# Dense output projection from layer two, and filler targets of 1.76 and 3.0 in turn, in a four-layer attention kernel

## The chip, the cores and the metric

The kernel runs on one core of a Trainium2 chip. The time is device microseconds of one launch, from the first instruction of the program to its end; the median of several runs is compared. A profile of one execution comes with it. The engines are named as the profile names them: PE (TensorE matmuls; PEld is its weight load), DVE (VectorE), ACT (ScalarE), POOL (GpSimd) and SP (SyncE, which here only issues DMAs).

## The reference

One sequence of 2048 rows and 640 columns goes through four residual attention layers. Layers one and three use the weights `A` and a sliding window of 256 keys; layers two and four use the weights `B` and attend to all 2048 keys, in both directions. There are 32 heads of 20 columns.

```python
def _A_ref(x, wqkv, wo):                 # _B_ref: the same without the mask
    qkv = (x @ wqkv).reshape(B, S, 3, H, Dh)...
    scores = jnp.einsum("bhqd,bhkd->bhqk", q, k) * (Dh ** -0.5)
    mask = (idx[:, None] - idx[None, :] >= 0) & (idx[:, None] - idx[None, :] < W)
    p = _softmax(jnp.where(mask, scores, -1e9))
    o = jnp.einsum("bhqk,bhkd->bhqd", p, v)
    return o.transpose(0, 2, 1, 3).reshape(B, S, D) @ wo

x = A_x
x = x + _A_ref(_layernorm(x), A_wqkv, A_wo)
x = x + _B_ref(_layernorm(x), B_wqkv, B_wo)
x = x + _A_ref(_layernorm(x), A_wqkv, A_wo)
x = x + _B_ref(_layernorm(x), B_wqkv, B_wo)
```

## The kernel before

**Tiling.** The 2048 rows are four chunks `c` of 512. The 32 heads are eight groups `g` of four; a head's 20 rows of Q and K lie at the partitions 32j to 32j+19, so that the four heads of a group use the four row strips of the PE array. A *unit* is one chunk's queries of one group in one layer (in the code layers count from `l` = 0). A unit's scores come out transposed, keys on partitions: one *bank* is 128 keys by 512 queries of one head. A *tile* is up to three banks (two and three in turn in layer one and the first part of layer two), and is one step of the main loop: PE computes the scores of a tile into one of two PSUM regions (line 1244), ACT takes the exponential (line 1275), and PE multiplies groups of four banks, two or three steps old, with V (line 1308) into the PSUM bank `op`. V has a 21st column of ones, so the 21st row of a head's strip in `op` is the sum of its weights. There are 1635 steps.

**Tail of a unit.** When a unit's last PV group is emitted, DVE copies `op` to `oT` (line 830) and the task `t_tail` is started: PE gathers the sums (line 1011), DVE takes reciprocals and splits them in two bf16 halves, PE transposes them (line 1028), PE spreads them over the strips (line 1039), and DVE multiplies (line 1043) into the slot `on[:, g, :]` of the chunk's tile `on`. Steps are left between these by `yield ("wait", 2)`. In `on`, as in `op`, a head has 32 partitions, of which 20 hold values; so a chunk's output projection contracts over eight blocks of 128 partitions, and the weights `wop` are laid out the same way by `load_wop` (lines 129 to 132), with zeros between, written once at the start by `t_zeros`.

**Output projection.** After the tail of group 7, `t_out(l, c)` (line 517 on) runs for each of four blocks of 128 rows and two halves of 320 columns eight matmuls (line 532), and DVE adds the result to the residual `x_sb` (line 541). `wop` is one buffer: when the next projection in the fixed order `out_seq` needs the other weights, the end of `t_out` loads them with four DMAs on SP. In the last chunk of layer four the first six groups are projected early by `t_before_last` (line 563), and `t_out` adds the last two.

**Background tasks.** Norms (`t_ln`), projections to Q, K and V (`project`, line 353; `t_v`, line 446), output projections and tails are Python generators. Each step of the main loop grants credit, `pump` (called with the rate of `rate(t)`) advances the tasks by it in order of need, and one PSUM bank (bank 6 after the first part of layer two) serves all of them. Their DMAs and instructions stand in each engine's queue in the order of the steps. SP's queue holds the loads of later units (one for V, four each for Q and K, or eight for a windowed unit) and the loads of `wop`; POOL's holds the loads of the projection weights and the stores of Q, K and V.

**Filler matmuls.** `keep_clock` (after `pump`, in each step) issues `unread`: a matmul of 128 by 128 by 512 into the free bank, whose result nothing reads (line 611). It does so while `state["heat"]`, what the tasks of this step have added, plus a carry of up to 3.0, is below `state["least"]`. A full projection matmul adds 1.0, an output matmul 0.64. The target is set once per step, and is zero from the second chunk of layer four on:

```python
warmth = 1.76 if state["unit"] >= woven else 1.0
state["least"] = warmth * n_b / 3 if state["unit"] < index[3, 1, 0, None] else 0.0
```

`woven` is the first unit of layer two, which begins among layer one's. When the free bank was used in the same step, no filler is issued. Two fillers stand ahead of each transpose group in the norms of the first two layers.

Of the kernel before, what the change touches and what calls it, by code (L numbers as in the profile page):

```python
# [12 lines left out]
ALU = mybir.AluOpType  # L13
ACT = mybir.ActivationFunctionType

P = 128
# [3 lines left out]
DH = 20  # L20
NT = S // P
KD = D // P
G = 8
C = 512
NC = S // C
EPS = 1e-5
SCALE = DH ** -0.5
HD = D // 2
# [21 lines left out]
def kernel(  # L50
# [10 lines left out]
    nc = tc.nc  # L61
# [27 lines left out]
    wo_in = (A_wo, B_wo)  # L89
# [5 lines left out]
    wop = big.tile([P, G, D], BF16, name="wop", tag="wop")  # L95
# [13 lines left out]
    op = ps[:, 7, :]  # L109
# [10 lines left out]
    for h in range(2):  # L120
        for n in range(2):
            a = n * D + h * HD
# [3 lines left out]
        nc.sync.dma_start(out=x_sb[:, 4 * c : 4 * c + 4, :], in_=xin[:, 4 * c : 4 * c + 4, :])  # L126
    nc.sync.dma_start(out=wv_sb[1][:], in_=wq_view[1][:, :, 2 * D : 3 * D])

    def load_wop(w):
        v = wo_in[w].rearrange("(g j e) f -> j e g f", g=G, j=4)  # L130
        for j in range(4):
            nc.sync.dma_start(out=wop[32 * j : 32 * j + DH, :, :], in_=v[j])
# [3 lines left out]
        out=ident[:], in_=ident[:], compare_op=ALU.not_equal, fill=1.0,  # L136
# [6 lines left out]
    for m, b, ge in (  # L143
# [4 lines left out]
        v = masks[:, m, b * P : (b + 1) * P]  # L148
        nc.gpsimd.affine_select(
            out=v, in_=v, compare_op=ALU.is_ge if ge else ALU.is_gt, fill=0.0,  # L150
# [26 lines left out]
    state = {"tick": 0, "held": None, "credit": 0.0, "early": True, "act": True, "unit": 0, "heat": 0.0, "carry": 0.0, "least": 0.0}  # L177
# [339 lines left out]
    out_seq = [0] * 4 + [1, 0] * 4 + [1] * 4  # L517
    out_n = [0]

    def t_out(l, c):  # L520
        on = ons[l, c]
        last = (l, c) == (3, NC - 1)
        while last and "before_last" not in ready:
            yield ("wait", 1)
        assert out_seq[out_n[0]] == l % 2
        for qb in range(4):
            for i in range(2):
                mb = yield from take_m()
                yp = ps[:, mb, 0:HD]
                g0 = G - 2 if last else 0  # L530
                for g in range(g0, G):
                    nc.tensor.matmul(  # L532
                        yp, lhsT=on[:, g, qb * P : (qb + 1) * P],
                        rhs=wop[:, g, i * HD : (i + 1) * HD],
                        start=(g == g0), stop=(g == G - 1),
                    )
                    if g < G - 1:
                        yield ("hold", 0.14)
                xv = x_sb[:, 4 * c + qb, i * HD : (i + 1) * HD]
                had = part_o["t"][:, 2 * qb + i, 0:HD] if last else xv  # L540
                nc.vector.tensor_tensor(out=xv, in0=had, in1=yp, op=ALU.add)  # L541
                drop_m(mb)
                yield ("pe", 0.14)
            if l < 3:
                stats(l + 1, c, qb)
            else:
                nc.sync.dma_start(out=xout[:, 4 * c + qb, :], in_=x_sb[:, 4 * c + qb, :])
        ons.pop((l, c))
        ready.add(("out", l, c))
        ready.add(("x", l + 1, c))  # L550
        n = out_n[0] = out_n[0] + 1
        if n < len(out_seq) and out_seq[n] != out_seq[n - 1]:
            load_wop(out_seq[n])

    def t_before_last():

        on = ons[3, NC - 1]
        for qb in range(4):
            for i in range(2):
                mb = yield from take_m()  # L560
                yp = ps[:, mb, 0:HD]
                for g in range(G - 2):
                    nc.tensor.matmul(
                        yp, lhsT=on[:, g, qb * P : (qb + 1) * P],
                        rhs=wop[:, g, i * HD : (i + 1) * HD],
                        start=(g == 0), stop=(g == G - 3),
                    )
                    if g < G - 3:
                        yield ("hold", 0.14)
                xv = x_sb[:, 4 * (NC - 1) + qb, i * HD : (i + 1) * HD]  # L570
                nc.vector.tensor_tensor(
                    out=part_o["t"][:, 2 * qb + i, 0:HD], in0=xv, in1=yp, op=ALU.add
                )
                drop_m(mb)
                yield ("pe", 0.14)
        ready.add("before_last")
# [420 lines left out]
    def t_tail(l, c, g, on, oT):  # L997
        def fill(count):

            for n in range(count * ((l, c, g) == (3, NC - 1, G - 1))):  # L1000
                nc.tensor.matmul(
                    ps[:, 0, :], lhsT=ident[:], rhs=masks[:, 0, :], start=True, stop=True
                )

        yield ("wait", 2)
        fill(2)
        mb = yield from take_m()
        warm_bank(mb)
        zp = ps[:, mb, 0:16]
        for qb in range(4):  # L1010
            nc.tensor.matmul(
                zp[:, 4 * qb : 4 * qb + 4], lhsT=oT[:, qb * P : (qb + 1) * P],
                rhs=sel4[:], start=True, stop=True,
            )
        rz = rzp.tile([P, 16], F32, name="rz", tag="rz")
        nc.vector.reciprocal(out=rz[:], in_=zp)
        drop_m(mb)

        hl = rzp.tile([P, 2, 16], BF16, name="hl", tag="hl")
        nc.vector.tensor_copy(out=hl[:, 0, :], in_=rz[:])  # L1020
        nc.vector.tensor_tensor(out=hl[:, 1, :], in0=rz[:], in1=hl[:, 0, :], op=ALU.subtract)
        yield ("pe", 0.25)
        fill(3)
        yield ("wait", 2)
        mb = yield from take_m()
        warm_bank(mb)
        rp = ps[0:32, mb, :].bitcast(BF16)[:, 0:P]
        nc.tensor.transpose(out=rp, in_=hl[:].rearrange("p n r -> p (n r)"), identity=ident[:])
        rT = rzp.tile([32, P], BF16, name="rT", tag="rT")
        nc.vector.tensor_copy(out=rT[:], in_=rp)  # L1030
        drop_m(mb)
        yield ("pe", 0.1)
        fill(1)
        yield ("wait", 2 if state["tick"] < last_tick[0] else 1)
        mb = yield from take_m()
        warm_bank(mb)
        zb = ps[:, mb, :]
        for qb in range(4):
            nc.tensor.matmul(  # L1039
                zb[:, qb * P : (qb + 1) * P], lhsT=spread4[:, qb, :], rhs=rT[:],  # L1040
                start=True, stop=True,
            )
        nc.vector.tensor_tensor(out=on[:, g, :], in0=oT[:], in1=zb, op=ALU.mult)  # L1043
        drop_m(mb)
        yield ("pe", 0.3)
        fill(3)
        ready.add(("tail", l, c, g))
        if (l, c, g) == (3, NC - 1, G - 3):
            push("before_last", t_before_last(), 0, 8.0)
        if g == G - 1:  # L1050
            need = first_use(l + 1, c, 0) if l < 3 else len(units) + c
            push(("out", l, c), t_out(l, c), need, 9.0)
            if l < 3:
                push_layer(l + 1, c)
    def t_zeros():

        z = ka_all[:, G : G + 4, :].rearrange("p a b -> p (a b)")
        yield ("wait", 4)
        for n in range(2):
            nc.gpsimd.dma_start(  # L1060
                out=wop[:, 4 * n : 4 * n + 3, :].rearrange("p g f -> p (g f)"), in_=z[:, 0 : 3 * D]
            )
            nc.gpsimd.dma_start(out=wop[:, 4 * n + 3, :], in_=z[:, 0:D])
            yield ("wait", 1)
        load_wop(0)
        for t in (*kts, *qts):
            nc.gpsimd.dma_start(out=t[:], in_=z[:, 0 : t.shape[1]])
            yield ("wait", 1)
        ready.add("kts")
# [67 lines left out]
    with tc.manual_schedule():  # L1137
# [9 lines left out]
        woven = index[1, 0, 0, PARTS[1][0]]  # L1147
# [4 lines left out]
        n = 0  # L1152
# [54 lines left out]
        t = -1  # L1207
        ended = None
        closed = -2
        while ended is None or t < ended + 8:  # L1210
# [3 lines left out]
            if t < len(tiles) or banks:  # L1214
# [26 lines left out]
                for n in range(2):  # L1241
                    for i, (u, j, m, b0, subs, first, last, end) in enumerate(cur):
                        for kc, q0, qn, col in subs[n : n + 1]:
                            nc.tensor.matmul(  # L1244
                                sp[:, i, col * P : (col + qn) * P],
                                lhsT=u.k(kc, j), rhs=u.q(j, q0, qn), start=True, stop=True,
# [22 lines left out]
                i = 0  # L1269
                while i < n_b:  # L1270
                    b0 = cur[i][3]
                    k = i
                    while k < n_b and cur[k][3] == b0:
                        k += 1
                    nc.scalar.activation(  # L1275
                        out=pt[:, i:k, b0 * P :], in_=sp[:, i:k, b0 * P :],
                        func=ACT.Exp, scale=SCALE,
                    )
                    i = k
                for i, b in enumerate(cur):  # L1280
                    pts.append((t, pt, i, b))
                warmth = 1.76 if state["unit"] >= woven else 1.0
                state["least"] = warmth * n_b / 3 if state["unit"] < index[3, 1, 0, None] else 0.0
                load_ahead()
                r = rate(t)
# [6 lines left out]
            for n in range(2 if n_b == 0 or t > closed + 1 else 0):  # L1292
# [7 lines left out]
                subs, end = group[0][3][4], group[-1][3][7]  # L1300
                first, last = group[0][3][5:7]
# [3 lines left out]
                for m, (kc, q0, qn, col) in enumerate(subs):  # L1305
                    for _, pg, i, b in group:
                        j = b[1]
                        nc.tensor.matmul(  # L1308
                            op[32 * j : 32 * j + VW, q0 * P : (q0 + qn) * P],
                            lhsT=u.v(kc, j), rhs=pg[:, i, col * P : (col + qn) * P],  # L1310
                            start=(first and m == 0), stop=(last and m == len(subs) - 1),
                            skip_group_check=u.windowed,
                        )
                if end and u.aside:
                    pair = side_done(u)
                    for n, j in enumerate(u.aside):
# [15 lines left out]
            if t > 0 and masked is not None:  # L1332
                cur_, pt_ = masked
                i = 0
                while i < len(cur_):
# [4 lines left out]
                    if m is not None:  # L1340
# [44 lines left out]
```

## Time and profile before

| | |
|---|---|
| median of 3 runs (range) | 2338.6 us (2338.2 to 2338.93) |
| the profiled execution's time | 2338.93 us |
| its span, first to last instruction | 2337.2 us |
| mean granted clock of PE | 0.852 |
| exponentials, ACT line 1275, 128x1536 | 1366 records, 1886.3 us |
| scores, PE line 1244, 512 columns | 4008 records, 644.6 us |
| output projection, PE line 532 | 976 records, 165.5 us, 312 ns each |
| fillers, PE line 611 | 672 records (768 weight loads), 231.7 us, 393 ns each |
| tail's product, DVE line 1043 | 128 records, 87.5 us, 683 ns each |

The profile's page gives busy time by engine and in 40 slices of the span; PEclk is the clock that PE was granted, in tenths of full speed. A matmul's busy time holds its pipeline, so matmuls that follow each other overlap and their mean durations add to more than the time they take; start to start is the price. In the timeline a bracket gives the idle time before an instruction and what ended it. An engine's queue is in order: an instruction that waits holds up all behind it.

### The profile page before, as it was taken

How to read it: one execution, taken by the hardware profiler on the slowest of the kernel's cores; microseconds unless marked ns; L12 is line 12 of the kernel's file. 1: busy time of each engine (PE TensorE's matmuls, PEld its weight loads, DVE VectorE, ACT ScalarE, POOL GpSimd, SP SyncE). 2: the span in 40 equal slices, each digit the busy share in tenths (PEclk: the TensorE clock that was granted, in tenths of full speed). 3: DMA queues.
4: the chain of work that ended last, by engine and by line, in shares of the span. 5: the costliest groups of instructions: out<-in, count | busy, mean ns of one | idle time of the engine just before them, and what ended most of it. 6: DMA issues, size and time to landing. Idle time of an engine off the chain costs nothing.

```text
span 2337.2 us, 40427 instructions
## 1 busy us (share of the span) xinstructions
PE 1992.5 (85%) x15613; PEld 722.9 (31%) x15773; DVE 1464.3 (63%) x2724; ACT 2179.5 (93%) x1753; POOL 271.1 (12%) x445
## 2 busy tenths in 40 slices
PE   8899988888888888888888898888888888888887
PEld 3444333333223332323323333333322222222222
DVE  6677775426646666656667644452577777777772
ACT  7788989899999988999899999999999999999997
POOL 3332311200200112001120013001000000000000
PEclk9999999999989999999999999999855565556556
DMA  5232321321300223102231023112210010011100
GB/s 183 81 103 80 107 65 56 90 68 48 89 21 25 58 68 90 43 14 58 70 99 31 17 82 107 41 28 76 65 30 27 26 38 27 27 35 39 31 14 12
DMA packets 84881, 132.57 MB, mean 57 GB/s; under 512 B 19760, under 2 KB 60080, under 8 KB 84688
## 3 DMA queue, kind: packets, MB, share of 16 engines
q1 hardware_dynamic: 65472, 76.80, 11.9%
q0 software_dynamic: 19216, 53.17, 7.8%
q8 instruction: 124, 2.03, 0.4%
q14 instruction: 69, 0.57, 0.1%
HBM read 98.70 MB, written 27.79 MB: 54 GB/s over the span
## 4 chain that ended last, share of the span: by engine, by line
ACT 40%; PE 27%; issue 17%; DVE 13%; DMA 1%; POOL 1%; ACTq 0%; SPq 0%; DVEq 0%; POOLq 0%; another core or an unknown queue 0%
ACT pt L1275 39%; PE ps L1244 7%; PE ps L353 5%; PE ps L532 4%; PE ps L1308 4%; DVE pt L1344 3%; PE ps L446 2%; PE ps L611 2%; DVE on L1043 1%; DVE st L304 1%; DMA wqk<-in_B_wqkv_dram 1%; ACT ka L1275 1%; DVE oT L830 1%; DVE raw_o L878 1%; PE ps L410 1%
## 5 line engine op out<-in xcount | busy, mean ns | idle before, releaser
L1275 ACT ACTIVATE pt<-ps 128x1536 bf16<-128x1536 f32 (+2 forms) x1641 | 2100.9, 1492 | 115.2 <-PE ps L1244 104.6
L1244 PE MATMUL ps<-qt,kt 32*128 32x512 bf16 x4008 | 644.6, 457 | 197.1 <-ACT pt L1275 164.2
L1308 PE MATMUL ps<-pt,vt 128*21 128x512 bf16 x3860 | 469.2, 458 | 5.1 <-issue 2.2
L1244 PEld LDWEIGHTS <-kt 32*128 32x128 bf16 x4008 | 191.0, 93 | 615.1 <-issue 592.0
L1344 DVE TENSOR_TENSOR pt<-pt,masks 128x1024 bf16<-128x1024 bf16 (+5 forms) x403 | 239.0, 626 | 131.5 <-ACT pt L1275 131.0
L611 PE MATMUL ps<-masks,ident 128*128 128x512 bf16 x672 | 231.7, 393 | 27.0 <-DVE rT L1030 9.6
L353 PE MATMUL ps<-xnT,wqk 128*128 128x512 bf16 x767 | 211.4, 388 | 24.8 <-DMA wqk<-in_B_wqkv_dram 4.2
L1308 PEld LDWEIGHTS <-vt 128*21 128x21 bf16 x3960 | 100.0, 90 | 319.1 <-issue 309.7
L304 DVE CAST st<-ps 128x512 bf16<-128x512 f32 x127 | 87.8, 691 | 154.4 <-PE ps L353 150.8
L532 PE MATMUL ps<-wop,on 128*128 128x320 bf16 x976 | 165.5, 312 | 6.9 <-DVE x_sb L541 2.5
L1244 PE MATMUL ps<-qa,ka 32*128 32x384 bf16 (+2 forms) x1408 | 116.8, 275 | 33.9 <-ACT pt L1275 28.8
L878 DVE TENSOR_SCALAR xnT<-ps 128x512 int32<-128x512 f32 x88 | 60.8, 691 | 106.3 <-PE ps L871 105.9
L1043 DVE TENSOR_TENSOR on<-oT,ps 128x512 bf16<-128x512 bf16 x128 | 87.5, 683 | 59.5 <-PE ps L1039 59.2
L830 DVE CAST oT<-ps 128x512 bf16<-128x512 f32 x112 | 76.9, 686 | 70.8 <-PE ps L1308 45.4
L446 PE MATMUL ps<-wv,xnT 128*128 128x320 bf16 x640 | 111.9, 309 | 7.0 <-DVE va L304 1.6
L541 DVE TENSOR_TENSOR x_sb<-x_sb,ps 128x320 bf16<-128x320 bf16 x120 | 57.9, 482 | 95.1 <-PE ps L532 94.9
L532 PEld LDWEIGHTS <-on 128*128 128x128 bf16 x976 | 90.2, 101 | 71.4 <-issue 38.4
L353 PEld LDWEIGHTS <-wqk 128*128 128x128 bf16 x830 | 71.3, 98 | 114.0 <-issue 49.2
L387 POOL TENSOR_SCALAR rstd<-mv 128x4 f32<-128x4 f32 x15 | 4.0, 265 | 815.6 <-DVE mv L374 815.5
L611 PEld LDWEIGHTS <-ident 128*128 128x128 bf16 x768 | 56.4, 97 | 126.2 <-issue 123.0
L1308 PE MATMUL ps<-pt,va 128*21 128x384 bf16 (+2 forms) x1408 | 77.6, 281 | 4.9 <-DVE pt L1344 2.9
L1244 PEld LDWEIGHTS <-ka 32*128 32x128 bf16 x1408 | 44.4, 92 | 101.2 <-issue 92.7
(107 smaller groups left out, 1790.9 us busy)
## 6 DMA issues: line engine op xcount, KB each, us to landing
vt<-v_d SPq DMA_DIRECT2D x48, 336.0 KB
kt<-k_d SPq DMA_DIRECT2D x192, 80.0 KB
wqk<-in_B_wqkv_dram POOLq DMA_DIRECT2D x80, 160.0 KB, 3.8
wqk<-in_A_wqkv_dram POOLq DMA_DIRECT2D x70, 160.0 KB, 3.3
k_d<-st POOLq DMA_DIRECT2D x75, 128.0 KB, 2.1
q_d<-st POOLq DMA_DIRECT2D x75, 128.0 KB, 2.1
qt<-q_d SPq DMA_DIRECT2D x384, 20.0 KB
v_d<-vs POOLq DMA_DIRECT2D x16, 336.0 KB, 3.1
```

The costliest lines, as they stand in the source:

```text
L304: nc.vector.tensor_copy(out=out_, in_=in_)
L353: nc.tensor.matmul(pq, lhsT=wt[:, dc, :], rhs=xt[:, dc, :], start=(dc == 0), stop=(dc == KD - 1),)
L446: nc.tensor.matmul(pv, lhsT=xt[:, dc, i * P : (i + 1) * P], rhs=wv_sb[l % 2][:, dc, h * HD : (h + 1) * HD], start=(dc == 0), stop=(dc == K ...
L532: nc.tensor.matmul(yp, lhsT=on[:, g, qb * P : (qb + 1) * P], rhs=wop[:, g, i * HD : (i + 1) * HD], start=(g == g0), stop=(g == G - 1),)
L611: nc.tensor.matmul(ps[:, b, :], lhsT=ident[:], rhs=masks[:, 0, :], start=True, stop=True)
L830: nc.vector.tensor_copy(out=oT[:], in_=op)
L878: V.tensor_scalar(out=xi.bitcast(I32)[:, i * C : (i + 1) * C], in0=side["psum"], scalar1=SCALE * LOG2E * E23, scalar2=127.0 * E23, op0=ALU ...
L1043: nc.vector.tensor_tensor(out=on[:, g, :], in0=oT[:], in1=zb, op=ALU.mult)
L1244: nc.tensor.matmul(sp[:, i, col * P : (col + qn) * P], lhsT=u.k(kc, j), rhs=u.q(j, q0, qn), start=True, stop=True,)
L1275: nc.scalar.activation(out=pt[:, i:k, b0 * P :], in_=sp[:, i:k, b0 * P :], func=ACT.Exp, scale=SCALE,)
L1308: nc.tensor.matmul(op[32 * j : 32 * j + VW, q0 * P : (q0 + qn) * P], lhsT=u.v(kc, j), rhs=pg[:, i, col * P : (col + qn) * P], start=(first ...
L1344: nc.vector.tensor_tensor(out=pt_[:, i:k, b0 * P :], in0=pt_[:, i:k, b0 * P :], in1=mv_, op=ALU.mult,)
```

## The change

From layer two on, the output projection contracts over five dense blocks of 128 rows in place of eight padded ones. `load_wop` gets a flag: dense weights come in one DMA of 128 partitions; once, after layer one, four further DMAs bring groups 6 and 7 of `B_wo` in the padded layout to the blocks 6 and 7. In `t_tail` the product is written to one of three scratch slots (5 to 7 of `on`), and two steps later SP copies each of the four heads' 20 rows to its dense place in the slots 0 to 4; a head that crosses a block's border takes two copies. The last two groups of the last chunk stay padded, and `t_before_last` contracts over four blocks (the last of 96 rows) in place of six. In `keep_clock`'s target, 1.76 becomes 3.0 on odd steps. A tail counts as done two steps later where it copies.

```diff
+    def packed(l, c):
+        return l > 0
+
-    def load_wop(w):
+    def load_wop(w, dense):
+        if dense:
+            nc.sync.dma_start(out=wop[:, 0:KD, :], in_=wo_in[w].rearrange("(b p) f -> p b f", p=P))
+            if w and out_n[0] == 4:
+                v = wo_in[w].rearrange("(g j e) f -> j e g f", g=G, j=4)
+                for j in range(4):
+                    nc.sync.dma_start(
+                        out=wop[32 * j : 32 * j + DH, G - 2 : G, :], in_=v[j][:, G - 2 : G, :]
+                    )
+            return
...
+        dense = packed(l, c) and not last
+        a, b = (0, KD) if dense else (G - 2 if last else 0, G)
         for qb in range(4):
             for i in range(2):
                 mb = yield from take_m()
                 yp = ps[:, mb, 0:HD]
-                g0 = G - 2 if last else 0
-                for g in range(g0, G):
+                for g in range(a, b):
                     nc.tensor.matmul(
                         yp, lhsT=on[:, g, qb * P : (qb + 1) * P],
                         rhs=wop[:, g, i * HD : (i + 1) * HD],
-                        start=(g == g0), stop=(g == G - 1),
+                        start=(g == a), stop=(g == b - 1),
                     )
...
-        if n < len(out_seq) and out_seq[n] != out_seq[n - 1]:
-            load_wop(out_seq[n])
+        if n < len(out_seq) and (n == 4 or out_seq[n] != out_seq[n - 1]):
+            load_wop(out_seq[n], n >= 4)
...
-                for g in range(G - 2):
+                for b in range(4):
+                    n = min(P, (G - 2) * 80 - b * P)
                     nc.tensor.matmul(
-                        yp, lhsT=on[:, g, qb * P : (qb + 1) * P],
-                        rhs=wop[:, g, i * HD : (i + 1) * HD],
-                        start=(g == 0), stop=(g == G - 3),
+                        yp, lhsT=on[0:n, b, qb * P : (qb + 1) * P],
+                        rhs=wop[0:n, b, i * HD : (i + 1) * HD],
+                        start=(b == 0), stop=(b == 3),
                     )
...
-        nc.vector.tensor_tensor(out=on[:, g, :], in0=oT[:], in1=zb, op=ALU.mult)
+        end = (l, c) == (3, NC - 1) and g >= G - 2
+        spread = packed(l, c) and not end
+        nu = on[:, 5 + g % 3 if spread else g, :]
+        nc.vector.tensor_tensor(out=nu, in0=oT[:], in1=zb, op=ALU.mult)
         drop_m(mb)
         yield ("pe", 0.3)
         fill(3)
+        if spread:
+            yield ("wait", 2)
+            for j in range(4):
+                r, a = (4 * g + j) * DH, 0
+                while a < DH:
+                    b, o = divmod(r + a, P)
+                    n = min(DH - a, P - o)
+                    nc.sync.dma_start(
+                        out=on[o : o + n, b, :], in_=nu[32 * j + a : 32 * j + a + n, :]
+                    )
+                    a += n
...
-        load_wop(0)
+        load_wop(0, False)
...
-                warmth = 1.76 if state["unit"] >= woven else 1.0
+                warmth = (3.0 if t % 2 else 1.76) if state["unit"] >= woven else 1.0
```

By line of the two built programs, the matmuls of the output projection falls from 976 to 712, the early part of the last one from 48 to 32, and the fillers rise from 768 to 1035. SP's list gains 423 copies within `on` and loses 23 loads of `wop`. The other counts are the same.

More of the change, by code (lines that the diff above doesn't have):

```diff
@@ L534, in t_out @@
                         rhs=wop[:, g, i * HD : (i + 1) * HD],
-                        start=(g == g0), stop=(g == G - 1),
+                        start=(g == a), stop=(g == b - 1),
                     )
-                    if g < G - 1:
+                    if g < b - 1:
                         yield ("hold", 0.14)
@@ L561, in t_before_last @@
                 yp = ps[:, mb, 0:HD]
-                for g in range(G - 2):
+                for b in range(4):
+                    n = min(P, (G - 2) * 80 - b * P)
                     nc.tensor.matmul(
-                        yp, lhsT=on[:, g, qb * P : (qb + 1) * P],
-                        rhs=wop[:, g, i * HD : (i + 1) * HD],
-                        start=(g == 0), stop=(g == G - 3),
+                        yp, lhsT=on[0:n, b, qb * P : (qb + 1) * P],
+                        rhs=wop[0:n, b, i * HD : (i + 1) * HD],
+                        start=(b == 0), stop=(b == 3),
                     )
-                    if g < G - 3:
+                    if b < 3:
                         yield ("hold", 0.14)
```

## The prediction

> **What bounds the kernel now.** I read the page's busy shares first, then its slices, then the busy time of each engine by stretches.
>
> ```profile
> PE 1992.5 (85%) x15613; PEld 722.9 (31%) x15773; DVE 1464.3 (63%) x2724; ACT 2179.5 (93%) x1753; POOL 271.1 (12%) x445
> ...
> ACT  7788989899999988999899999999999999999997
> ...
> PEclk9999999999989999999999999999855565556556
> ```
>
> ScalarE (ACT), which takes the exponentials, is the bound: 2179.5 of 2337.2 us. The change leaves its instructions as they are, so it can only move the 157.7 us in which ACT idles. The stretches say where these lie (span, then busy us and count for PE, PEld, DVE, ACT, POOL, then granted clock, DMA share, GB/s):
>
> ```profile
> 486.00:529.00 43.00, 36.15 (x289) 13.98 (x293) 13.85 (x37) 43.00 (x34) 0.00 (x0) 1.00 0.21 60
> 564.00:578.00 14.00, 11.02 (x72) 4.24 (x72) 9.22 (x17) 10.33 (x8) 3.77 (x7) 0.63 0.28 60
> ...
> 673.00:687.00 14.00, 13.64 (x68) 2.67 (x66) 7.10 (x10) 11.25 (x8) 0.00 (x0) 0.51 0.01 1
> ...
> 855.00:902.00 47.00, 41.33 (x330) 15.75 (x333) 28.99 (x48) 41.78 (x31) 18.23 (x26) 1.00 0.41 122
> ...
> 1532.00:1557.00 25.00, 22.92 (x196) 10.63 (x195) 10.73 (x29) 23.32 (x18) 0.00 (x0) 1.00 0.00 1
> ...
> 1890.00:1917.00 27.00, 24.02 (x179) 10.18 (x176) 20.93 (x34) 22.34 (x18) 0.00 (x0) 0.84 0.14 41
> ```
>
> Four kinds of stretch. In 486:529 the filler matmuls run at clock 1.00 and ACT never idles. In 564:578 and 673:687 the clock fell to a half for some microseconds and ACT idled 3.67 and 2.75 us; ten such dips between 486 and 1400 us idle ACT 24.5 us together (the others: 1.62, 3.42, 2.98, 2.36, 0.86, 2.20, 2.63, 1.97, by the same view). In 855:902 the projections make PE late at full clock (5.2 us). And each output projection makes ACT wait: 1.7 us at 1532:1557, 4.66 us at 1890:1917 in layer four, where there are no fillers and the clock rests at a half.
>
> What makes a dip is seen in the fillers alone, by 3.4 us stretches before the one at 673.4 (PE busy, PEld, clock, DMA, GB/s):
>
> ```profile
> 659.70:663.10 3.40, 1.60 (x5) 0.32 (x5) 1.00 0.67 203
> 663.10:666.50 3.40, 0.98 (x3) 0.38 (x4) 1.00 0.29 77
> 666.50:670.00 3.50, 1.37 (x4) 0.31 (x4) 1.00 0.15 41
> 670.00:673.40 3.40, 0.77 (x2) 0.19 (x2) 1.00 0.00 0
> ```
>
> Five, three and four fillers held the clock, two did not; before the dip at 994 it went 3, 3, 2. So the stretch itself was thin in full-array work, while a normalisation chain held the one spare PSUM bank.
>
> **The change by parts.** The sum is made on the profiled run's own 2338.93 us (span 2337.2 and 1.7 around it), 0.3 above the median of 2338.6.
>
> (1) *Fewer output matmuls in layer four.* Three projections go from 64 to 40 matmuls, the split last one from 48+16 to 32+16. The timeline of the second one:
>
> ```profile
> 1893.23 0.68 DVE L1043 TENSOR_TENSOR on<-oT,ps 128x512 bf16<-128x512 bf16 x1
> ...
> 1893.96 2.29 PE L532 MATMUL ps<-wop,on 128*128 128x320 bf16 x8 [0.45 <-DVE on L1043]
> ...
> 1897.26 1.97 PE L532 MATMUL ps<-wop,on 128*128 128x320 bf16 x8
> 1897.44 1.45 ACT L1275 ACTIVATE pt<-ps 128x1536 bf16<-128x1536 f32 x1 [1.91 <-PE ps L1244]
> ...
> 1899.99 1.45 ACT L1275 ACTIVATE pt<-ps 128x1536 bf16<-128x1536 f32 x1 [1.10 <-PE ps L1244]
> ...
> 1901.66 1.26 PE L532 MATMUL ps<-wop,on 128*128 128x320 bf16 x8
> ```
>
> Eight take 2.29 us cold and 1.26 us warm, so 0.28 and 0.157 us each. ACT idles 1.91 and 1.10 us at the first two groups, 1.65 at the rest. In the new kernel the first group of five waits for copies (part 3): I leave it 1.5 of its 1.91. The second is 3 x 0.28 = 0.85 shorter, leaving 0.25. Warm groups began 1.84 us apart (1899.82 and 1901.66), against ACT's 1.38 a tile; three fewer make 1.37, so the 1.65 goes. That is 4.66 - 1.75 = 2.9. The other two projections idle ACT 4.23 and 3.26: the three together 12.15 - 5.25 = 6.9 saved. The split one idles it 3.35 and loses two of six: 1. Sum -8; bounds 0 (the wait eats it) and -13.
>
> (2) *Fewer in layers two and three.* Eight projections lose 24 matmuls x 0.157 = 3.8 us of PE each, mostly beside idle PE: the densest, 1532:1557, idles ACT 1.7 us, the spaced ones about 0.5. 1.7 + 7 x 0.5 = 5.2 at most; I take -3, bounds -5 and 0.
>
> (3) *Copies and their wait.* Where line 1043 wrote its slot of `on`, it now writes a scratch slot, and SP issues 4 or 5 copies a tail: 423 in all, at 0.37 us apart (the loads' spacing in the timeline at 1911.55) 157 us of SP, which today mostly waits: 577 us at its value loads for one line of PE alone. Behind a waiting copy stand the loads of later units, a whole unit of 5 to 22 tiles ahead of need, so their delay of some 2 us is covered; without that cover each would cost that much. Loads of `wop` fall from 40 issues to 17; the next projection is at least twelve tiles (16 us) away. The output matmuls are issued on the same scheduling step as the last copies, two tiles after the broadcast matmul. A landing between SBUF places on SP is not in the trace; bounds are 2.1 us (stores of K from `st`) and 4.6 us (copies of zeros into `wop`, eight times the bytes). I take 2.1, the nearer in size. From the end of line 1043 the last copy lands at 1.1 + 2.1 + 0.1 = 3.3 us, which is 5.0 after the broadcast began (1892.22; line 1043 ends at 1893.91). PE reaches the fifth matmul, the first that needs these rows, at 2.7 + 4 x 0.157 = 3.3. So PE stands 1.7 us at full clock; scores, PV and projections wait behind it. ACT has two tiles in hand, 2.76 us; 1.7 + 0.8 (five matmuls) + 0.7 (PV and scores, 0.3 each with issue) = 3.2, so ACT idles 0.4: eight times, +3. With 4.6 us it is 2.9 each, +23; below, 0, since the old path had a wait here too (0.45).
>
> (4) *More fillers.* The built program has 1035 in place of 768. At full clock one filler put 0.32 us between scores and PV (1006.17 to 1006.49) and two 0.54, so one more is 0.22: 59 us of PE. Of the 267, 164 lie where neither a projection nor an output runs, 32 beside outputs: there ACT is full and PE has slack. A tile with three takes 0.97 + 2 x 0.22 = 1.41 us against ACT's 1.38, but the neighbour has one or two and scores have two PSUM regions, so free; uncovered, 0.03 x some 400 odd three-bank tiles is 12 us. The other 71 stand in the two-bank stage and beside projections, where PE is the later: up to 71 x 0.22 = 15.6. I take half, +7, since the step places them only when nothing else is due; bounds 0 and +16.
>
> (5) *Fewer dips.* Of the 24.5 us, four dips (673, 902, 994, 1192; 10.7 us) lie in filler or tail stretches, where the fillers grow by a quarter to a half; the rest follow output projections and norms, where few are added (2 to 5, 0 to 1) and the dense form takes full-array work away. Some of these shorten as well; I take half of all, -12, bounds -24 and +6 (two new dips at about 3).
>
> Here a rule speaks against the change. The Trainium skill ("TensorE: Matmul & The Clock Gate", section on HAM oscillation) says in effect that the clock falls when PE idles for more than some 3.4 us between matmuls. In the stretch before the dip at 673.4 PE was busy 2.29 of 3.40 us, with no gap over 1.2 us, so here the trace differs: full-array work decided. By the rule fillers in a busy stream would buy nothing, part 5 would be 0 and the sum -1.
>
> Sum: -8 - 3 + 3 + 7 - 12 = -13, so 2338.9 - 13 = 2326 us.
>
> **Rivals.** *The dips stay (2338 us).* Tails hold the spare bank on the steps where filler is missing, and a filler can't go there. For: the dip at 994 had two overlapping chains. Against: a quarter more filler beside them. Without part 5 the sum is -1. *The dips vanish (2314 us).* For: windows that held had three or more fillers, and odd tiles now ask for three. Against: those after norms. -13 - 12 = -25. *The copies are late (2356 us).* One mechanism, at twelve projections: SBUF copies land at 4.6 us as into `wop`; PE stands 2.5 us longer and ACT with it, 12 x 2.5 = 30 on top of 2326. It decides from 13 / 12 = 1.1 us more, so from 3.2 us of landing. For: the copies into `qt` took 9.7. Against: those were early, in a busy queue and six times larger.
>
> **How the numbers follow.** A measurement of this kernel tells about 0.2% (4.7 us) from no change. Forecast (2316 to 2334) 0.45, dips vanish 0.17, dips stay 0.20, copies late 0.18. The first two are faster (0.62), the third the same, the last slower. The time is the likeliest case's, 2326. The range takes in most of the neighbours: 2304 (dips gone and projections at their low bound) to 2346 (copies between the bounds).
>
> **What would show it.** Part 1: ACT idle at layer four's projections of about 2 us each in place of 4.66. Part 3: the fifth output matmul waiting for a copy into `on`, 1 to 2 us. Part 4: ACT still full in filler stretches. Part 5: the half-clock time between 486 and 1400 us, now 78 us, at about 40. It is wrong if that time has not fallen, or if PE's waits for the copies exceed 3 us.

## The result and the profile after

| | before | after |
|---|---|---|
| median of 4 runs each (range) | 2338.76 us (2338.2 to 2343.15) | 2361.89 us (2355.39 to 2364.41) |
| the profiled execution's time, its span | 2338.93, 2337.2 us | 2360.69, 2359.0 us |
| mean granted clock of PE | 0.852 | 0.843 |

The change makes the kernel slower: the ratio is 1.0091, with an interval of 1.0066 to 1.0115. That is 23 us more, where 13 us less were forecast, and 16 us above the range.

The page of the changed kernel, the same lines as before:

```profile
PE 2032.5 (86%) x15591; PEld 708.2 (30%) x15760; DVE 1463.2 (62%) x2724; ACT 2181.2 (92%) x1753; POOL 273.8 (12%) x445
...
ACT  7788989899999889999899889989999999999997
...
PEclk9999999999999889999999989989755565556556
```

ACT's busy time is unchanged (2181.2 against 2179.5), so the whole loss is ACT's idle time: 177.8 us of the span in place of 157.7. Its digit 8 now stands at more places of layers two and three, and PEclk is 9 down to 8 at four slices in place of one.

The stretches of the changed kernel (span, busy us and count for PE, PEld, DVE, ACT, POOL, then clock, DMA share, GB/s). The first three are those shown before; the last two are output projections, one of layer three and the one of layer four shown before at 1890:

```profile
486.00:529.00 43.00, 36.88 (x293) 14.19 (x297) 13.87 (x37) 43.00 (x34) 0.00 (x0) 1.00 0.26 69
564.00:578.00 14.00, 13.11 (x106) 5.29 (x102) 10.52 (x20) 13.28 (x11) 0.00 (x0) 0.88 0.07 17
673.00:687.00 14.00, 13.01 (x94) 4.12 (x96) 5.07 (x7) 14.00 (x12) 0.00 (x0) 1.00 0.06 13
...
1043.00:1057.00 14.00, 10.70 (x75) 3.58 (x75) 6.21 (x12) 10.59 (x9) 0.00 (x0) 0.88 0.03 8
...
1914.00:1941.00 27.00, 22.21 (x149) 7.55 (x146) 19.92 (x33) 21.69 (x17) 0.00 (x0) 0.70 0.14 43
```

In these stretches the fillers did their part. At 564 the clock is 0.88 in place of 0.63 and ACT idles 0.72 us in place of 3.67; at 673 the dip is gone and ACT is full. The loss is at the projections: 3.4 of 14 us at 1043, and at 1914 ACT still idles 5.3 us, where the prediction had about 2.

The waits of the changed kernel name the cause (engine, line, what it waited for; us in total, times, longest):

```profile
PE ps L546 <- DMA on<-on: 18.4, 8, 3.0
...
PEld L546 <- DMA on<-on: 5.8, 2, 3.4
```

PE stands (it is idle, held by a wait) before the fifth output matmul, as the prediction said, but longer. The projection at 1043 in the timeline (start, us, engine, line, operation; in brackets the idle time before it and its releaser):

```profile
1043.34 0.69 DVE L1061 TENSOR_TENSOR on<-oT,ps 128x512 bf16<-128x512 bf16 x1 [0.36 <-PE ps L1054]
...
1044.06 3.33 SPq L1072 DMA_DIRECT2D on<-on  x4
...
1045.28 0.79 PE L546 MATMUL ps<-wop,on 128*128 128x320 bf16 x4
...
1048.76 0.30 PE L546 MATMUL ps<-wop,on 128*128 128x320 bf16 x1 [2.69 <-DMA on<-on]
...
1049.32 0.50 PE L1273 MATMUL ps<-qt,kt 32*128 32x512 bf16 x3
...
1049.74 1.51 PE L546 MATMUL ps<-wop,on 128*128 128x320 bf16 x5
1049.91 1.45 ACT L1304 ACTIVATE pt<-ps 128x1536 bf16<-128x1536 f32 x1 [2.32 <-PE ps L1273]
...
1052.45 4.13 ACT L1304 ACTIVATE pt<-ps 128x1536 bf16<-128x1536 f32 x3 [1.08 <-PE ps L1273]
```

The product (line 1061) ends at 1044.03. SP needs until 1047.39 to issue four copies. Four output matmuls run at once, the fifth stands 2.69 us, and the scores that ACT needs stand behind it, so ACT idles 2.32 us. The next group of five takes 1.51 us in place of the 0.84 or so of a warm one: the clock fell at 1049.5, 0.7 us after the stand, and ACT idles another 1.08 us. In layer four, with the clock at rest already, the first gap grew as well, from 1.91 us to 3.08:

```profile
1917.90 3.03 SPq L1072 DMA_DIRECT2D on<-on  x4
...
1922.31 0.43 PE L546 MATMUL ps<-wop,on 128*128 128x320 bf16 x1 [2.31 <-DMA on<-on]
...
1923.93 1.45 ACT L1304 ACTIVATE pt<-ps 128x1536 bf16<-128x1536 f32 x1 [3.08 <-PE ps L1273]
...
1926.45 9.51 ACT L1304 ACTIVATE pt<-ps 128x1536 bf16<-128x1536 f32 x7 [1.07 <-PE ps L1273]
```

The second gap, 1.07 us, is about what it was (1.10), where the sum had 0.25. Only behind it did the thinner projection pay as planned: seven exponentials without a gap.

To see where the time went over the whole kernel, I lined up the two traces by step of the main loop, which is the same list of tiles in both, and added ACT's gaps from 2 us before to 8 us after each projection. The granted clock has two values in these traces, 1.0 and 0.5; time at half clock is the time at 0.5:

| steps | before, us (at half clock) | after, us (at half clock) |
|---|---|---|
| 0 to 304, two banks | 448.7 (10.2) | 447.1 (3.4) |
| 304 to 1152, layers two and three and the start of four | 1179.4 (78.5) | 1205.2 (119.5) |
| 1152 to 1632, layer four | 676.0 (588.4) | 672.8 (602.1) |
| ACT idle at the eight projections of layers two and three | 8.7 | 35.3 |
| ACT idle at the four of layer four | 17.0 | 14.5 |

The 26.6 us more at eight projections are as much as the 25.8 us by which the middle part grew; gains and losses elsewhere cancel. One projection makes the comparison by chance: that of the third chunk in layer four begins 5.5 us after its product ended, because the bank was busy (a matmul of line 886 and its reader, line 893, hold it), and PE finds the copies landed. There ACT idles 0.9 us, against 4.2 before.

### The profile page after: what moved, and what is told of

It reads as the page before. It is cut to its first block, busy times and chain, and to the rows that moved or that the text cites. A ratio compares the mean times of both kernels' runs of the same rounds, so it can differ in the third digit from the quotient of the medians.

```text
span 2359.0 us, 41085 instructions
## 1 busy us (share of the span) xinstructions
PE 2032.5 (86%) x15591; PEld 708.2 (30%) x15760; DVE 1463.2 (62%) x2724; ACT 2181.2 (92%) x1753; POOL 273.8 (12%) x445
## 4 chain that ended last, share of the span: by engine, by line
ACT 37%; PE 30%; DVE 15%; issue 14%; DMA 2%; SPq 1%; POOL 1%; ACTq 0%; DVEq 0%; POOLq 0%
ACT pt L1304 35%; PE ps L1273 8%; PE ps L366 5%; PE ps L1337 5%; PE ps L626 3%; PE ps L546 3%; DVE pt L1373 3%; PE ps L459 3%; DVE on L1061 1%; DVE st L317 1%; DMA on<-on 1%; DMA wqk<-in_B_wqkv_dram 1%; PE ps L423 1%; DVE oT L845 1%; ACT ka L1304 1%
## 5 line engine op out<-in xcount | busy, mean ns | idle before, releaser
L1337 PE MATMUL ps<-pt,vt 128*21 128x512 bf16 x3860 | 474.6, 463 | 3.6 <-issue 0.8
L1273 PEld LDWEIGHTS <-kt 32*128 32x128 bf16 x4008 | 186.1, 94 | 587.9 <-issue 568.5
L626 PE MATMUL ps<-masks,ident 128*128 128x512 bf16 x935 | 301.2, 385 | 41.7 <-DVE rT L1045 10.5
L546 PE MATMUL ps<-wop,on 128*128 128x320 bf16 x712 | 134.5, 323 | 32.3 <-DMA on<-on 18.4
L626 PEld LDWEIGHTS <-ident 128*128 128x128 bf16 x1035 | 78.4, 97 | 157.2 <-issue 137.5
L546 PEld LDWEIGHTS <-on 128*128 128x128 bf16 x712 | 64.6, 102 | 92.6 <-issue 64.4
L522 POOL DMA_DIRECT2D k_d<-st x75 | 42.6, 568 | 299.0 <-DVE st L317 257.4
```

Of the source, the lines that this page charges most:

```text
L546: nc.tensor.matmul(yp, lhsT=on[:, g, qb * P : (qb + 1) * P], rhs=wop[:, g, i * HD : (i + 1) * HD], start=(g == a), stop=(g == b - 1),)
L626: nc.tensor.matmul(ps[:, b, :], lhsT=ident[:], rhs=masks[:, 0, :], start=True, stop=True)
L1273: nc.tensor.matmul(sp[:, i, col * P : (col + qn) * P], lhsT=u.k(kc, j), rhs=u.q(j, q0, qn), start=True, stop=True,)
L1337: nc.tensor.matmul(op[32 * j : 32 * j + VW, q0 * P : (q0 + qn) * P], lhsT=u.v(kc, j), rhs=pg[:, i, col * P : (col + qn) * P], start=(first ...
```

## The experiments

Each ratio is to the kernel before, run on the same chip. Its median was 2343.2 us beside the first four runs, 2345.1 beside the next four and 2338.5 beside the last two, so kernels of different groups are compared by ratio; us worked out from a ratio are that ratio times 2339. Stage times come from the one profiled execution of a kernel. Two questions were asked first: which half of the change costs the time, and is it the copies' lateness (A), the projection thinned to five blocks (B), or fillers in PE's way (C)?

**Only the targets.** The kernel before, with the new target alone.

```diff
-                warmth = 1.76 if state["unit"] >= woven else 1.0
+                warmth = (3.0 if t % 2 else 1.76) if state["unit"] >= woven else 1.0
```

> The kernel before with the filler target of 3.0 on odd steps alone; padded projection, no copies. Theory A (copies land late: PE stands 1.7 to 3.0 us at eleven of twelve dense projections, and the thin stretch then drops the clock): none of that here, and the dips of the filler stretches go, so faster than before by 8 to 15 us, some 2324 to 2331. Theory B (40 full-array matmuls in place of 64 leave the stretch too thin): the same as A here. Theory C (three fillers on odd steps make PE late): slower than before, 2345 to 2362.

Measured: 2334.09 us, ratio 0.9953 (0.9935 to 0.9971). The page of this kernel:

```profile
PEclk9999999999999999999999999999855565556556
```

No slice of the middle part is below 9; time at half clock there is 37.5 us in place of 78.5. The fillers gain 11 us, and C falls.

**Only the dense form.** The changed kernel, with the old target.

```diff
-                warmth = (3.0 if t % 2 else 1.76) if state["unit"] >= woven else 1.0
+                warmth = 1.76 if state["unit"] >= woven else 1.0
```

> The changed kernel with the filler target of before, 1.76 on every step. Theory A: the waits stay and the filler stretches' dips come back, 2362 to 2375. Theory B: the same, or worse, since fewer fillers stand beside the thinner projection. Theory C: back near before, 2335 to 2345.

Measured: 2365.43 us, 1.0091 (1.0074 to 1.0107). The dense form alone is as slow as the whole change. The gain of the first run doesn't add to it: half-clock time in the middle part falls from 139.9 us here to 119.5 in the changed kernel, and that part takes 1206.3 and 1205.2 us.

**Projection four steps later.** The copies get time to land before the output matmuls are issued.

```diff
+            if g == G - 1 or (l, c, g) == (3, NC - 1, G - 3):
+                yield ("wait", 4)
         ready.add(("tail", l, c, g))
```

> The changed kernel with four more steps between the last copies of a chunk and its output projection, and nothing else. Theory A: PE's wait for the copies, 32 us in all, falls below 3 us, and with it the dips that begin there: 2330 to 2342. Theory B: the projection is as thin as before and the dips stay: 2352 or more. Theory C: no change, about 2360.

Measured: 2338.7 us, 0.9975 (0.9959 to 0.9991). No output matmul waits for a copy any more, and 1.2% of the time is back.

**Five blocks without copies.** The kernel before with the new targets, its projections from layer two on taken over the first five of the eight padded blocks (four of six in the early part of the last one).

```diff
-                for g in range(g0, G):
+                g1 = KD if l and not last else G
+                for g in range(g0, g1):
...
-                for g in range(G - 2):
+                for g in range(4):
```

> The kernel before with the filler target of 3.0 on odd steps, and its output projections from layer two on contract over the first five of eight padded blocks (four of six in the early part of the last): three blocks of the contraction are left out. The thinner projection without the copies. Theory A: no wait, so 2320 to 2332. Theory B: the dips at the projections are there without any copy, 2350 or more. Theory C: slower than before, as the changed kernel.

Measured: 2316.67 us, 0.9888 (0.9867 to 0.9908). The thinner projection as such isn't slow; B falls as the cause. (The profiled execution took 2323.7 us, the other three 2315.3 to 2316.7, so the stage times of this kernel are of an untypical one.) But the run before, without waits too, was 0.9% behind this one. Two causes were open: its projections came six steps later in all (L), or the 423 copies cost something by themselves (M).

**Five blocks, late.** The kernel without copies, its tails and projections moved to the steps of the late projection.

```diff
+        if l and not ((l, c) == (3, NC - 1) and g >= G - 2):
+            yield ("wait", 2)
+            if g == G - 1 or (l, c, g) == (3, NC - 1, G - 3):
+                yield ("wait", 4)
```

> The kernel with five of eight padded blocks and no copies (three blocks left out; 0.989 of before), but its tails and projections stand at the steps of the one with the late projection: every tail two steps longer, the last of a chunk six. Theory L (what the late projection still loses to the five blocks, 0.9 per cent, is its lateness: norms and projections come too close to their use): 0.995 to 0.999 of before. Theory M (it is the 423 copies themselves, by their load on SP and the DMA engines): 0.987 to 0.991 of before.

Measured: 2336.81 us, 0.9965 (0.9948 to 0.9981). That is the value with copies on this schedule (0.9975) within the intervals: the schedule costs 0.8%, and the copies' load 0.1% with some 0.2% to either side, so none that the runs show.

**Two queues.** The changed kernel, with the copies of heads 1 and 3 issued on POOL.

```diff
-                    nc.sync.dma_start(
+                    (nc.gpsimd if j % 2 else nc.sync).dma_start(
```

> The changed kernel with the second and fourth head's copies issued by POOL instead of SP. Theory A (the wait is the chain of four issues of 0.72 to 0.76 us on one queue, then the landing): two chains side by side end 1.5 us earlier, PE's wait falls from 2.4 to about 1 us at a place and the time to 0.998 to 1.004 of before. Rival (the landing of an SBUF copy is late by itself, whatever the queue, or POOL's issue is as slow and stands behind the weights' loads): the wait stays above 2 us and the ratio at 1.007 or more.

Measured: 2334.16 us, 0.9963 (0.9945 to 0.998). The waits of this kernel:

```profile
PE ps L546 <- DMA on<-on: 4.4, 7, 1.1
PEld L546 <- DMA on<-on: 4.2, 6, 1.3
```

Its copies in the view of the tile `on` (least/median/most ns of an issue, first and last start):

```profile
L1072 SPq DMA_DIRECT2D on<-on x212: 554/717/852, 492.5 to 2269.5; - x106
L1072 POOL DMA_DIRECT2D on<-on x211: 499/511/1022, 492.6 to 2269.5; - x106
```

And POOL's copies among the DMA issues (KB each, us from issue to landing):

```profile
on<-on POOLq DMA_DIRECT2D x165, 20.0 KB, 1.7
```

The projection shown above at 1043, in the timeline of this kernel:

```profile
1036.35 0.69 DVE L1061 TENSOR_TENSOR on<-oT,ps 128x512 bf16<-128x512 bf16 x1 [0.36 <-PE ps L1054]
...
1037.07 1.47 SPq L1072 DMA_DIRECT2D on<-on  x2
1037.33 1.01 POOL L1072 DMA_DIRECT2D on<-on  x2 [4.46 <-DVE on L1061]
...
1040.13 0.30 PE L546 MATMUL ps<-wop,on 128*128 128x320 bf16 x1 [0.75 <-DMA on<-on]
```

The issues end 1.5 us after the product in place of 3.4, and PE stands 0.75 us in place of 2.69. PE's longest wait for the copies on line 546 falls from 3.0 to 1.1 us with the schedule untouched. A copy on POOL lands 1.7 us after its issue, less than the 2.1 of the sum; for those on SP the changed kernel's waits fit the 2.1 (below). So what was late in the changed kernel is the chain of four issues. The Trainium skill ("Perfetto Trace Analysis", DMA Optimizations) says that balancing transfers over the engines that can issue them may help where descriptor generation is the limit. This run agrees, with 1.28% of the time between the two kernels.

**Dense in layer four alone**, with the projection four steps later there.

```diff
     def packed(l, c):
-        return l > 0
+        return l == 3
...
-            if w and out_n[0] == 4:
+            if w and out_n[0] == 12:
...
-        if n < len(out_seq) and (n == 4 or out_seq[n] != out_seq[n - 1]):
-            load_wop(out_seq[n], n >= 4)
+        if n < len(out_seq) and out_seq[n] != out_seq[n - 1]:
+            load_wop(out_seq[n], n >= 12)
...
+            if g == G - 1 or (l, c, g) == (3, NC - 1, G - 3):
+                yield ("wait", 4)
```

> Dense projection in layer four alone, started four steps after its last copies, with the filler target of 3.0 on odd steps; layers two and three as before. If the parts add: the odd-step target's 0.5 per cent and layer four's 9 us, so 0.990 to 0.993 of before. If the dense form's gain in layer four was a matter of the whole schedule: 0.995 or more.

Measured: 2324.58 us, 0.9921 (0.9897 to 0.9946). That lies in the range for parts that add. The middle part takes 1176.2 us, layer four 665.6, against 676.0 before.

**Projection two steps later**, in place of four.

```diff
+            if g == G - 1 or (l, c, g) == (3, NC - 1, G - 3):
+                yield ("wait", 2)
         ready.add(("tail", l, c, g))
```

> The changed kernel with the projection two steps later in place of four. Two steps are 2.7 us and the wait was 1.7 to 3.0 us. Theory A: nearly all of it is gone, waits of at most 0.5 us. Theory L: less late, so faster than with four steps: 0.993 to 0.997 of before. Theory M: as with four steps, 0.997 to 0.999.

Measured: 2334.78 us, 0.9955 (0.9932 to 0.9978). Two steps are enough to take the wait away. The projection shown above at 1043, in the timeline of this kernel:

```profile
1028.80 17.58 ACT L1306 ACTIVATE pt<-ps 128x1536 bf16<-128x1536 f32 x13
...
1031.39 0.69 DVE L1061 TENSOR_TENSOR on<-oT,ps 128x512 bf16<-128x512 bf16 x1 [0.36 <-PE ps L1054]
...
1032.11 3.33 SPq L1072 DMA_DIRECT2D on<-on  x4
...
1036.01 1.10 PE L546 MATMUL ps<-wop,on 128*128 128x320 bf16 x5
```

And the 14 us about it, in the view by stretches:

```profile
1034.00:1048.00 14.00, 12.79 (x100) 4.70 (x100) 6.03 (x14) 14.00 (x12) 0.00 (x0) 1.00 0.02 4
```

The same copies take the same 3.33 us on SP, but the output matmuls start 4.6 us after the product began in place of 1.9, and five run in a row. The clock stays at 1.00 and ACT runs thirteen exponentials without a gap.

**Two steps later, old targets.**

```diff
+            if g == G - 1 or (l, c, g) == (3, NC - 1, G - 3):
+                yield ("wait", 2)
...
-                warmth = (3.0 if t % 2 else 1.76) if state["unit"] >= woven else 1.0
+                warmth = 1.76 if state["unit"] >= woven else 1.0
```

> Dense projection everywhere from layer two, two steps later than in the changed kernel, with the filler target of before (1.76 on every step). With 3.0 on odd steps the same kernel was at 0.9955. If the odd-step target is worth with the dense form what it was worth with the padded one (0.5 per cent): 0.999 to 1.002. If it is worth nothing beside the dense form, as between the changed kernel and its twin with 1.76 (both 1.0091): 0.994 to 0.997.

Measured: 2322.51 us, 0.993 (0.9907 to 0.9954). Beside the dense form the fillers of the odd steps are worth nothing, and perhaps cost a quarter of a per cent: the intervals of this run and the last overlap. Half-clock time in the middle part is 71.7 us in both.

**No steps before the copies.** The changed kernel without the two steps between product and copies, so that product and output matmuls are issued on one step.

```diff
         if spread:
-            yield ("wait", 2)
             for j in range(4):
```

> The changed kernel without the two steps that each tail gives its copies: they stand right behind the product, and the projection starts two steps sooner. Theory A: the copies land no sooner, so PE stands 2.7 us longer at each of twelve projections, 4 to 6 us in all each; 1.015 to 1.03 of before. Theory L alone (only lateness costs): at or below the changed kernel's 1.009.

Measured: 2382.09 us, 1.0183 (1.015 to 1.0217). Its waits:

```profile
PE ps L546 <- DMA on<-on: 35.5, 11, 4.2
...
PEld L546 <- DMA on<-on: 7.6, 2, 4.3
```

A longer wait costs more, and this closes the chain. The four kernels of the next table differ in the wait and, but for the two queues, in the steps of the projection. The steps alone work the other way: without copies, later ones cost time (0.9888 against 0.9965), while here the latest kernel is one of the two fast ones and the earliest is the slowest. I summed PE's longest stand in the first group of each dense projection, and ACT's gaps as above:

| kernel | PE's stands, us | ACT idle at eight projections, us | half clock in the middle part, us | profiled execution, us | ratio |
|---|---|---|---|---|---|
| two steps later | none over 0.25 | 9.5 | 71.7 | 2327.5 | 0.9955 |
| two queues | 5.8 | 14.4 | 85.3 | 2329.7 | 0.9963 |
| the change | 26.3 | 35.3 | 119.5 | 2360.7 | 1.0091 |
| no steps before the copies | 38.8 | 46.6 | 136.5 | 2385.3 | 1.0183 |

All columns rise together. The first 5.8 us of standing, at most 1.1 at a place, cost little: the two ratios agree within their intervals. That ACT had work in hand for so long is my explanation. From there on each microsecond costs between one and two of the kernel's time: (1.0091 - 0.9963) x 2339 = 30 us for 20.5 more, and (1.0183 - 1.0091) x 2339 = 22 for 12.5 more; the intervals leave about 7 and 10 us to either side.

## Why the prediction was wrong

**The step that failed is part 3, the copies and their wait, put at +3 us.** Between the changed kernel and the one that only starts the projection two steps later lie (1.0091 - 0.9955) x 2339 = 32 us. That is 29 of the 36 us between the forecast's -13 and the measured +23. The rest is of the size of parts 4 and 5, together put at -5: beside the dense form the new target was worth nothing (1.0091 with it and without). The mechanism of part 3 was named rightly (the fifth output matmul waits for the last copy, and scores queue behind it); three sizes in it were off, and a fourth cost had no term.

- *The spacing of the issues.* I took 0.37 us from loads of the same 20 KB out of memory. The tile view of the changed kernel has the copies:

```profile
L1072 SPq DMA_DIRECT2D on<-on x423: 554/712/1640, 488.6 to 2299.0; - x141
```

  Median 0.71 us, about twice as much, and 0.76 from start to start. So the last copy is issued 2.3 to 2.7 us after the product ends, where the sum had 1.1. From that issue to the release of PE nine of eleven take 1.9 to 2.2 us, which is the 2.1 + 0.1 of the sum: the landing was right. (At two projections it took 3.5, beside loads of projection weights on POOL.) The Trainium skill ("DMA: Bandwidth & Descriptors", Anatomy of one DMA) gives a fixed cost of some 2.0 us for a DMA issued from GpSimd; these waits on SP's copies agree with that size, while the copies that POOL itself issued in the run with two queues landed after 1.7 us.
- *So PE stands longer.* The stands at eleven projections add to 26.3 us, 2.4 each, where the sum had 1.7.
- *What a stand costs ACT.* I credited ACT with two tiles in hand, 2.76 us. At the eight projections of layers two and three it had 0.93 to 1.87 us left when the stand began, 1.5 in the mean, since the tiles had been running while the first four output matmuls went by. The first gap behind the stand is then 0.9 to 2.5 us, 15.7 in all, where the sum had 0.4 each.
- *What came after it.* The rest of the 35.3 us are gaps in the next tiles, most of them of 0.4 to 1.2 us. At six of the eight the clock fell to a half 0.4 to 1.7 us after the stand had ended, as at 1049.5 above; the two without a fall idle ACT 2.3 and 3.6 us, the six 2.6 to 6.5. The windows of the eight hold 33.2 us of half clock. With the same five-block projection and no stand they hold 10.0 (two steps later; 5.7 to 13.6 over the five such kernels), and with two queues, on the schedule of the change, 11.6. So the stand, and not the thinner projection, brings most of the falls there. The prediction had no term for this.

The rule that I weighed against part 5 returns here. The Trainium skill ("TensorE: Matmul & The Clock Gate", HAM oscillation) describes a kernel whose PE waits for a DMA in each round and falls to the half clock. Here falls followed stands of 2.1 to 3.0 us, below the 3.4 us that the page gives, in a stream that was thin around them; stands of 1.7 and 2.7 us at the other two were not followed by one.

What decides shows when the trace of the changed kernel is cut on a grid. All its falls lie on one of 3.413 us, and each lasts one or more such windows. Here are two windows over the stand from 539.41 to 542.08, without a fall, and two about the one from 1046.07 to 1048.76, in the view by stretches:

```profile
537.48:540.89 3.41, 1.80 (x13) 0.64 (x10) 1.93 (x3) 3.41 (x3) 0.00 (x0) 1.00 0.13 30
540.89:544.30 3.41, 2.22 (x20) 0.90 (x20) 0.94 (x3) 1.17 (x2) 0.00 (x0) 1.00 0.04 11
...
1046.09:1049.50 3.41, 0.74 (x8) 0.29 (x8) 0.41 (x2) 1.50 (x2) 0.00 (x0) 1.00 0.08 18
1049.50:1052.91 3.41, 3.41 (x17) 0.92 (x14) 2.80 (x7) 1.91 (x2) 0.00 (x0) 0.50 0.02 5
```

The two stands are equally long, but the first is split over two windows, with PE busy 1.80 and 2.22 us, and the second lies in one, with 0.74. At the six projections with a fall the window before it had PE busy 0.7 to 1.4 us. So where a stand lies on the grid counts too, beside its length. PE's busy time isn't the whole rule: the window before the dip at 673 had 2.29 us.

**The rival "the copies are late"** (2356 us, chance 0.18) was the right case with the wrong cause: I had it decide by the landing, and it came by the issues. Its price of 2.5 us more of standing at twelve places was too high for the stand (0.7 more) and made up by what I had not counted.

**Part 1 (-8)** was the right size without the wait: layer four takes 668.7 us with the projection two steps later and 665.6 to 666.5 where it comes four steps later, against 676.0. In the changed kernel 3.2 us are left of it: at the second projection the first gap grew, the second stayed at 1.07, and only the later ones went.

**Part 2 (-3)** is seen at the projections only where they don't come later: ACT idles 10.9 us at the eight with the target alone and 4.4 with five blocks without copies, which differ in the thinner projection alone, though the middle part takes 1173 us in both. With the dense form two steps later and the old targets it is 8.7 us, as before. That kernel's middle part is 8.0 us shorter than before all the same (1171.4); by stretches of 48 steps it gains and loses up to 5 us, about 673 for one 3.9, and where this comes from was not traced.

**Part 4 (+7)** is seen from two sides. In stretches where ACT is full it is free, as said: steps 864 to 912 take 63.4 us in both kernels, with 102 fillers in place of 79. Beside the dense form without the wait, the new target costs 0.0025 x 2339 = 6 us, if that difference is real.

**Part 5 (-12)** had the right direction for the kernel before: parts 4 and 5 together were -5, and the target alone measured -11, interval -7 to -15. In the changed kernel the dips in filler and tail stretches shrank too (673 gone, 902 from 6.8 to 3.4 us of half clock, 994 from 10.2 to 3.4, 1192 unchanged at 6.8), but new and longer ones at projections and norms outweigh them. The sign that I had named, about 40 us of half clock between 486 and 1400 us in place of 78, came in the first run (34.1), and in the changed kernel the contrary (99.0). So did the other one, a wait of PE over 3 us (3.03 the longest, 3.4 on a weight load). The time at half clock by itself is a poor price, though: the middle part takes 1173.3 us with 37.5 us of it (the target alone) and 1171.4 with 71.7 (two steps later, old targets).

**What stays open.** Later projections cost time in themselves: 0.9888 against 0.9965 for the two kernels without copies. I take it that norms and projections to Q, K and V crowd together behind a later output projection; that was not tried alone. Nor is it settled why the gain of the new target and that of the dense form don't add. The fastest kernels that leave nothing out are dense in layer four alone (0.9921) and dense from layer two, two steps later, with the old target (0.993); the bound of 0.9888 was not reached by one.

## What to carry to other kernels

When one engine's matmul waits for the last of several DMAs, price the chain of issues on their queue from the same kind of transfer, source and destination, and not from the nearest load of equal size; then ask how much work the bound engine has in hand at the moment when the wait begins, not when its tile was started. Before giving up a layout for such a wait, start the consumer a step or two later or split the issues over two queues: here either took back 1.3 to 1.4%. A short stand of PE in a stretch with little matmul work can cost the clock afterwards too (here at six of eight places), so its price may be more than its length.

## What the runs showed of the hardware

A copy between places of SBUF holds SP's queue for 0.71 us (median of 423, of which 329 have 20 KB and the others are parts of one), where the 20 KB loads out of memory hold it for 0.32 to 0.36 (timeline of before at 1911.55). On POOL's queue the same copy takes 0.51 us to issue and lands 1.7 us after the issue began. The Trainium skill ("DMA: Bandwidth & Descriptors", SWDGE vs HWDGE vs iDMA) calls the setup of the hardware path, which SP uses, the faster one. By the length of the issue in the profile these copies say the contrary; spans on POOL are rough there, but the longer waits with all copies on SP go the same way.
